# Moving 128 rows of w_down into eight small late loads, and a back-edge mark on VectorE's loop, in a decode kernel that mixes attention and a feed-forward block

## The chip, the cores and the metric

The kernel runs on one core of one Trainium2 chip. The metric is the device time of one execution in microseconds (us); before the change it is 350.62 us, the median of three runs (350.5 to 350.71).

## The reference

One token `x` of 512 numbers goes through an attention block with cached keys and values and through a feed-forward block; a gate mixes the two results.

```python
g = _sigmoid((x * gate_w).sum(-1, keepdims=True))
a = _A_ref(x, A_k_cache, A_v_cache, A_wq, A_wo)   # 32 query heads, 8 K/V heads, 32768 positions, head size 128
b = _B_ref(x, B_w_gate, B_w_up, B_w_down)         # (silu(x @ w_gate) * (x @ w_up)) @ w_down, 512 -> 1792 -> 512
return g * a + (1 - g) * b
```

Everything is bf16. K and V together are 128 MiB, of 148.11 MB that are read in all. `w_down` has 1792 rows of 512 numbers (1 KB each).

## The kernel before

The code is written per engine, with semaphores set by hand; nothing is scheduled by a planner. All loads but two small ones (`x` and `gate_w`, on ScalarE's queue) are issued by SyncE (SP), in this order: `wq`, `w_gate`, `w_up`, then K and V of the eight K/V heads ("groups") in turn, then `w_down`, then `wo`. They go into five pages of 32 KB per partition: `PG_A`, `PG_B`, `PG_C` (0 to 2) hold K, two pages at a time, `PG_V` and the one above it V. The last V goes to `PG_B` and `PG_C`, whose K is used up first. SP waits in its own order until the page of the next load is free: for K on `sem_fill` (transposes done by TensorE), for V on `sem_v_free` (the matmuls with V done).

TensorE (PE) runs a start part, the loop over the groups and an end part. In the loop (`emit_k`) it transposes K, eight blocks to a unit (L348, `emit_fill`; sixteen units a group, each adds 1 to `sem_fill`, so that 128 means the last unit of the last group); VectorE copies each unit to SBUF (L712); PE multiplies it with the queries (L360, `emit_scores`). ScalarE makes the exponentials, and PE multiplies those of the group before with V (L417, `emit_v`).

The feed-forward block runs in the start part: gate and up products, the product `tmask`, and its transposition into columns by 14 matmuls with a vector of ones (L524), which VectorE copies to `tT` (L693). `w_down` lies as 14 consecutive rows to a partition, `wd[128, 14, 512]`, so column `j` of `tT` belongs to `wd[:, j, :]`:

```python
sp.dma_start(
    wd[:, :, :], B_w_down.rearrange("(p j) n -> p j n", j=FC)
).then_inc(sem_ld_wd, 16)
```

Its product stands in the end part (`emit_end`): after the last V product and its reduction, PE waits for `sem_ld_wd` and runs 14 matmuls of 128x1 by 128x512, `emit_strip` (L220), over four strips of one PSUM bank in turn, as partial sums onto which the first sixteen row blocks of `wo` are added. `wo` comes in five pieces (`WO_CUTS`, L340) of 16, 9, 4, 2 and 1 rows per partition, issued when the matmuls with the last but one V are done; PE uses the last four with `emit_rows` (L231) as they land. Behind the last piece VectorE copies the result row (L765), and SP and ScalarE store a half each.

Of the kernel before, what the change touches and what calls it, by code (L numbers as in the profile page):

```python
# [8 lines left out]
BF16 = mybir.dt.bfloat16  # L9
# [3 lines left out]
def bass_gated_mix__gqa_block_cached__swiglu_ffn__decode_kernel(  # L13
# [14 lines left out]
    G = A_k_cache.shape[1]  # L28
# [4 lines left out]
    F = B_w_gate.shape[1]  # L33
    NOUT = A_wo.shape[1]
# [3 lines left out]
    FC = F // 128  # L38
# [8 lines left out]
    UPG = NB * UPP  # L47
# [4 lines left out]
    STEP = 16  # L52
# [10 lines left out]
    NSTRIP = 4  # L63
# [5 lines left out]
    PG_A, PG_B, PG_C = 0, 1, 2  # L69
# [5 lines left out]
    NPG = 5  # L75
    assert G % 2 == 0

    with ExitStack() as es:
        def S_(name):
            return es.enter_context(nc.semaphore(name))  # L80
# [8 lines left out]
        sem_ld_x = S_("s_ld_x")  # L89
        sem_ld_g = S_("s_ld_g")  # L90
        sem_ld_wd = S_("s_ld_wd")
        sem_ones = S_("s_ones")
        sem_dc = S_("s_dc")
        sem_pz = S_("s_pz")
# [16 lines left out]
        sem_dve_tT = S_("s_dve_tT")  # L111
        sem_fill = S_("s_fill")
# [24 lines left out]
        def T(name, shape, dt):  # L137
            return es.enter_context(nc.sbuf_tensor(name, shape, dt))
# [5 lines left out]
        ones_bf = T("ones_bf", [128, 2], BF16)  # L144
# [8 lines left out]
        og_col = T("og_col", [128, 1], FP32)  # L153
        qblk = T("qblk", [128, (G + 2) * STEP], BF16)
        qcur = T("qcur", [128, 2, 2 * HPG], BF16)
        tT = T("tT", [128, FC], BF16)
        wd = T("wd", [128, FC, NOUT], BF16)
        page = T("page", [128, NPG, PAGE], BF16)
        ktT = T("ktT", [128, NKT, 2 * UW], BF16)
        ET = T("ET", [128, NT, HPG], BF16)  # L160
# [21 lines left out]
        ps_m = P("ps_m", [128, 512], FP32)  # L182
# [3 lines left out]
        M_P0 = M_B0 + HPG  # L186
        M_S0 = M_P0 + HPG
        M_T0 = M_S0 + HPG
        M_O0 = M_T0 + FC
        M_X0 = M_O0 + WOJ  # L190
        M_G0 = M_X0 + KC
        assert M_G0 + 1 <= 512
# [13 lines left out]
        tmask = ktT[:, 2, 0:F]  # L206
# [5 lines left out]

        wq_v = page[:, PG_Q, 0 : KC * H * DH].rearrange("p (c n) -> p c n", c=KC)
        wgu = page[:, PG_F, 0 : 2 * KC * F].rearrange("p (w c f) -> p w c f", w=2, c=KC)
        wo_v = page[:, PG_X, 0 : WOJ * NOUT].rearrange("p (j n) -> p j n", j=WOJ)
        qall = qblk[:, :].rearrange("p (g e c) -> p g e c", e=2, c=2 * HPG)

        def emit_strip(pe, w, vec, j, start, stop):
            c = j % NSTRIP
            return pe.matmul(  # L220
                ps_c[32 * c : 32 * c + 1, :],
                vec[:, j : j + 1],
                w[:, j, :],
                start=start,
                stop=stop,
                skip_group_check=True,
            )
# [32 lines left out]
        with nc.Block("main") as block:  # L260
# [25 lines left out]
            @block.sync  # L286
            def _(sp):
                def load_k(g):
                    lo = PG_A if g % 2 else PG_B
                    dst = page[:, lo : lo + NB, :].rearrange("p b (r d) -> p b r d", d=DH)  # L290
                    src = A_k_cache[0, g, :, :].rearrange("(p b r) d -> p b r d", b=NB, r=R)
                    if g > 1:
                        sp.wait_ge(sem_fill, UPG * (g - 1) + UPP)
                        sp.dma_start(
                            dst.rearrange("p b r d -> p (b r d)"),
                            src.rearrange("p b r d -> p (b r d)"),
                        ).then_inc(sem_k[0], 16)
                        return
                    for b in range(NB):
                        first = lo + b == PG_B  # L300
                        if g and first:
                            sp.wait_ge(sem_fill, UPP)
                        sp.dma_start(dst[:, b, :, :], src[:, b, :, :]).then_inc(
                            sem_k[0] if first else sem_k1 if g else sem_k[1], 16
                        )

                def load_v(g):
                    src = A_v_cache[0, g, :, :].rearrange("(p b r) d -> p b r d", b=NB, r=R)
                    if g == G - 1:
                        lo, sem = PG_L, sem_vl  # L310
                        sp.wait_ge(sem_fill, UPG * g + UPP)
                    else:
                        lo, sem = PG_V, sem_v
                        if g:
                            sp.wait_ge(sem_v_free, STEP * (g + 1))
                        else:
                            sp.wait_ge(sem_pe_h, 1)
                    sp.dma_start(
                        page[:, lo : lo + NB, :].rearrange("p b n -> p (b n)"),
                        src.rearrange("p b r d -> p (b r d)"),  # L320
                    ).then_inc(sem, 16)

                sp.dma_start(wq_v, A_wq.rearrange("(p c) n -> p c n", c=KC)).then_inc(sem_q, 16)  # L323
                for w, src in enumerate((B_w_gate, B_w_up)):
                    sp.dma_start(  # L325
                        wgu[:, w, :, :], src.rearrange("(p c) f -> p c f", c=KC)
                    ).then_inc(sem_f, 16)
                load_k(0)
                for g in range(1, G):
                    load_k(g)  # L330
                    load_v(g - 1)
                load_v(G - 1)
                sp.dma_start(
                    wd[:, :, :], B_w_down.rearrange("(p j) n -> p j n", j=FC)
                ).then_inc(sem_ld_wd, 16)
                sp.wait_ge(sem_v_free, STEP * G)
                src = A_wo.rearrange("(p j) n -> p j n", j=WOJ)
                for k, s in enumerate(sem_wo):
                    a, b = WO_CUTS[k], WO_CUTS[k + 1]
                    sp.dma_start(wo_v[:, a:b, :], src[:, a:b, :]).then_inc(s, 16)  # L340

            @block.tensor
            def _(pe):
# [103 lines left out]
                def emit_start():  # L447
                    pe.wait_ge(sem_r, 9)
                    pe.wait_ge(sem_ones, 2)
                    for n, (a, b) in enumerate(  # L450
                        ((r_row[:, 0, :], ones_f[0:1, :]), (ones_f[0:1, :], r_row[:, 1, :]))
                    ):
                        ins = pe.matmul(ps_i, a, b, start=(n == 0), stop=(n == 1))
# [4 lines left out]
                    for c in range(KC):  # L458
                        ins = pe.matmul(
                            ps_m[:, M_X0 + c : M_X0 + c + 1],  # L460
                            xv[:, c, :],
                            ones_bf[0:1, 0:1],
                            start=True,
                            stop=True,
                        )
# [4 lines left out]
                    for t in range(QT):  # L470
                        for c in range(KC):
                            for k in range(NSTRIP):
                                n = (t * NSTRIP + k) * QN
                                ins = pe.matmul(  # L474
                                    pst[0][32 * k : 32 * k + 1, t * QN : (t + 1) * QN],
                                    xT[:, c : c + 1],
                                    wq_v[:, c, n : n + QN],
                                    start=(c == 0),
                                    stop=(c == KC - 1),
                                    skip_group_check=True,  # L480
                                )
# [6 lines left out]
                        start=True,  # L488
                        stop=True,
# [6 lines left out]
                    for e in range(2):  # L496
                        for t in range(QT):
                            for j in range(NSTRIP):
# [4 lines left out]
                                    start=True,  # L503
# [15 lines left out]
                                )  # L519
                    ins.then_inc(sem_pe_h, 1)  # L520
                    pe.wait_ge(sem_dve_tm, 1)
                    tv = tmask.rearrange("p (m j) -> p j m", j=FC)
                    for j in range(FC):
                        ins = pe.matmul(  # L524
                            ps_m[:, M_T0 + j : M_T0 + j + 1],
                            tv[:, j, :],
                            ones_bf[:, 0:1],
                            start=True,
                            stop=True,
                        )  # L530
                    ins.then_inc(sem_pe_t, 1)
                    pe.wait_ge(sem_ps0, 1)
                    pe.wait_ge(sem_dve_tT, 1)
                    for n, sem in enumerate((sem_v_free, sem_red)):
                        c = M_P0 + HPG * n
                        pe.matmul(
# [16 lines left out]
                def emit_end():  # L553
                    emit_v(
                        [[(sem_exp, (G + 1) * STEP), (sem_vl, 16)], []], (PG_L, PG_L + 1)
                    )
                    pe.wait_ge(sem_rc, G * STEP)
                    emit_reduce((G + 1) * STEP)
                    pe.wait_ge(sem_ld_wd, 16)
                    for j in range(FC):  # L560
                        emit_strip(pe, wd, tT, j, j < NSTRIP, False)

                    pe.wait_ge(sem_dve_oT2, 1)
                    pe.matmul(
                        ps_m[:, M_O0 : M_O0 + WOJ], pmat[:, :], O2a[:, :], start=True, stop=True
                    ).then_inc(sem_pe_O2, 1)
                    pe.wait_ge(sem_dve_O2, 1)
                    emit_wo(pe, 0)
# [42 lines left out]
            def _(dve):  # L611
# [78 lines left out]
                    ALU.mult,  # L690
                ).then_inc(sem_dve_tm, 1)
                dve.wait_ge(sem_pe_t, 1)
                dve.tensor_copy(tT[:, :], ps_m[:, M_T0 : M_T0 + FC]).then_inc(sem_dve_tT, 1)  # L693

                def emit_out(i, at):
                    dve.wait_ge(sem_red, i + STEP)
# [8 lines left out]
                        ALU.mult,  # L705
                    ).then_inc(sem_rc, STEP)

                with dve.Fori(0, G * STEP, STEP) as i:
                    for n in range(UPG + 1):
                        if n < UPG:  # L710
                            dve.wait_ge(sem_fill, i + (n + 1))
# [47 lines left out]
        for k in range(1, len(sem_wo)):  # L759
            ins = emit_wo(pe, k)  # L760
# [37 lines left out]
```

## Time and profile before

| what | value |
|---|---|
| time, median of three runs | 350.62 us (350.5 to 350.71) |
| the profiled execution | 350.62 us, of it the span 349.3 us |
| mean granted clock of TensorE | 0.859 |
| busy: PE, weight loads of PE, VectorE, ScalarE | 258.6, 219.7, 186.3, 33.4 us |
| read from HBM | 148.11 MB, 424 GB/s over the span |
| `w_down`, issue to landing | 31.0 us |
| five pieces of `wo`, issue to landing | 18.2, 20.6, 21.4, 21.6, 21.5 us |

The span goes from the first to the last instruction of the program. Lines are named L and their number in the kernel before. "DMA share" is the mean busy share of the core's 16 DMA engines. Besides loads, the profile lists packets of kind "instruction", with which the engines' programs are fetched.

### The profile page before, as it was taken

The numbers are of one execution on the slowest core, as the hardware profiler recorded it, in microseconds if no ns is written. First come the engines' busy times: TensorE is split into PE (matmuls) and PEld (weight loads), VectorE is DVE, ScalarE is ACT, GpSimd is POOL, SyncE is SP. The second block draws the span as 40 slices with busy tenths as digits, with TensorE's granted clock in tenths as the row PEclk, the third lists the DMA queues.
The fourth block names the chain that finished last, engine by engine and source line by source line (L and its number), as shares of the span: only waits on it lengthen the run. The fifth ranks groups of instructions, "written<-read, shape, count | busy, mean of one in ns | idle before, by whom it ended". The sixth has DMA issues, their size and how long they took to land.

```text
span 349.3 us, 8833 instructions
## 1 busy us (share of the span) xinstructions
PE 258.6 (74%) x3915; PEld 219.7 (63%) x3915; DVE 186.3 (53%) x227; ACT 33.4 (10%) x143; POOL 2.8 (1%) x15
## 2 busy tenths in 40 slices
PE   1354994799749981999469982999479972999384
PEld 1124993799449941997259942996279842995241
DVE  4044994499229921697129921895139920894101
ACT  1002000300030003000400003000400012000400
POOL 3000000000000000000000000000000000000000
PEclk9996999599969987699859985898859995898878
DMA  8999999999999999999999999999999999999895
GB/s 321 417 461 420 418 430 462 453 413 428 420 443 443 428 435 443 428 443 413 435 450 428 435 413 435 450 435 428 420 435 450 428 428 420 443 443 428 388 427 236
DMA packets 3907, 148.22 MB, mean 424 GB/s; under 512 B 442, under 2 KB 572, under 8 KB 828
## 3 DMA queue, kind: packets, MB, share of 16 engines
q1 hardware_dynamic: 3892, 148.11, 98.5%
q8 instruction: 6, 0.10, 0.1%
q14 instruction: 1, 0.01, 0.0%
q10 hardware_dynamic: 8, 0.00, 0.0%
HBM read 148.11 MB, written 0.00 MB: 424 GB/s over the span
## 4 chain that ended last, share of the span: by engine, by line
DMA 61%; PE 34%; issue 2%; DVE 2%; SPq 1%; DVEq 0%
DMA page<-in_A_k_cache_dram 54%; PE pst L348 25%; DMA page<-in_A_wo_dram 6%; PE ps_sc L360 6%; DVE ktT L712 2%; PE ps_o L417 2%; SPq L340 0%; SPq L325 0%; DVE pmaxf L720 0%; PE ps_sc L231 0%; PE ps_m L401 0%; SPq L323 0%; PE ps_m L397 0%; DVE res_row L765 0%; DVE gm L730 0%
## 5 line engine op out<-in xcount | busy, mean ns | idle before, releaser
L712 DVE COPY ktT<-pst 128x2048 bf16<-128x2048 bf16 x128 | 153.4, 1221 | 66.0 <-PE pst L348 61.9
L348 PE MATMUL pst<-ident_f,page 128*128 128x128 f32 x1024 | 148.0, 300 | 40.1 <-DMA page<-in_A_k_cache_dram 37.6
L348 PEld LDWEIGHTS pst<-ident_f,page 128*128 128x128 f32 x1024 | 126.7, 155 | 44.4 <-DMA page<-in_A_k_cache_dram 38.2
L360 PEld LDWEIGHTS ps_sc<-qcur,ktT 128*128 128x128 bf16 x2048 | 64.0, 97 | 8.1 <-DVE ktT L712 7.1
L360 PE MATMUL ps_sc<-qcur,ktT 128*128 128x8 bf16 x2048 | 64.3, 166 | 6.4 <-DVE ktT L712 6.4
L417 PE MATMUL ps_o<-page,ET 128*16 128x512 bf16 x512 | 37.2, 456 | 6.0 <-DMA page<-in_A_v_cache_dram 6.0
L417 PEld LDWEIGHTS ps_o<-page,ET 128*16 128x16 bf16 x512 | 13.9, 103 | 25.5 <-issue 16.9
L599 ACT ACTIVATE ET<-ps_sc,nbias 128x128 bf16 x64 | 23.9, 556 | 52.6 <-DVE nbias L738 52.6
L592 ACT ACTIVATE acc<-ps_o 128x512 f32<-128x512 f32 x8 | 4.8, 597 | 221.2 <-PE ps_o L417 217.1
L730 DVE TENSOR_REDUCE gm<-ps_m 4x1 f32<-4x128 f32 x8 | 2.2, 278 | 39.4 <-PE ps_m L397 39.4
L599 ACT ACTIVATION_READ_ACCUMULATOR ET<-ps_sc,nbias 128x1 f32 x64 | 18.3, 285 | 0.0
L720 DVE TENSOR_REDUCE pmaxf<-ps_sc 128x4 f32<-128x512 f32 x16 | 11.0, 686 | 8.4 <-PE ps_sc L360 8.4
L474 PE MATMUL pst<-page,xT 128*1 128x512 bf16 x32 | 3.6, 627 | 9.1 <-DMA page<-in_A_wq_dram 9.1
L438 PE MATMUL ps_m<-sel,acc 128*128 128x4 f32 x64 | 8.4, 255 | 1.8 <-ACT acc L592 1.6
L438 PEld LDWEIGHTS ps_m<-sel,acc 128*128 128x128 f32 x64 | 7.7, 191 | 2.5 <-ACT acc L592 2.2
L401 PE MATMUL ps_m<-diag,ones_f 4*128 4x4 f32 x16 | 3.2, 268 | 6.9 <-DVE diag L734 6.9
L697 DVE RECIPROCAL rS<-ps_m 128x4 f32<-128x4 f32 x9 | 1.6, 182 | 12.4 <-PE ps_m L438 12.4
L401 PEld LDWEIGHTS ps_m<-diag,ones_f 4*128 4x128 f32 x16 | 2.7, 213 | 8.4 <-issue 8.4
L474 PEld LDWEIGHTS pst<-page,xT 128*1 128x1 bf16 x32 | 0.9, 115 | 10.9 <-issue 10.9
L650 DVE CAST ktT<-pst 128x1024 bf16<-128x1024 f32 x2 | 2.4, 1218 | 8.7 <-PE pst L474 8.7
L429 PEld LDWEIGHTS ps_m<-esum,ones_f 128*128 128x128 f32 x32 | 4.2, 190 | 3.5 <-issue 3.5
L429 PE MATMUL ps_m<-esum,ones_f 128*128 128x4 f32 x32 | 4.9, 258 | 0.0
(70 smaller groups left out, 48.5 us busy)
## 6 DMA issues: line engine op xcount, KB each, us to landing
page<-in_A_k_cache_dram SPq DMA_DIRECT2D x4, 4096.0 KB, 35.0
page<-in_A_wq_dram SPq DMA_DIRECT2D x1, 4096.0 KB, 13.5
page<-in_A_wo_dram SPq DMA_DIRECT2D x1, 2048.0 KB, 18.2
page<-in_B_w_gate_dram SPq DMA_DIRECT2D x1, 1792.0 KB, 17.4
page<-in_B_w_up_dram SPq DMA_DIRECT2D x1, 1792.0 KB, 21.2
wd<-in_B_w_down_dram SPq DMA_DIRECT2D x1, 1792.0 KB, 31.0
page<-in_A_wo_dram SPq DMA_DIRECT2D x1, 1152.0 KB, 20.6
page<-in_A_wo_dram SPq DMA_DIRECT2D x1, 512.0 KB, 21.4
```

The lines of the kernel that those rows point to most:

```text
L348: ins = pe.transpose(pst[u % NST][:, k * 128 : (k + 1) * 128], kv[:, n * 128 : (n + 1) * 128], ident_f[:, :],)
L360: ins = pe.matmul(ps_sc[b][:, col : col + 2 * HPG], kt[:, k, e, :], qcur[:, e, :], start=(e == 0), stop=(e == 1),)
L401: pe.matmul(ps_m[:, M_B0 : M_B0 + HPG], ones_f[0:HPG, :], diag[:, :], start=True, stop=True,).then_inc(sem_b, STEP)
L417: ins = pe.matmul(ps_o[32 * c : 32 * c + RQ * HPG, :], ET[:, n : n + RQ, :].rearrange("p n h -> p (n h)"), v[:, k * RQ : (k + 1) * RQ, :], ...
L429: pe.matmul(ps_m[:, M_S0 : M_S0 + HPG], ones_f[:, :], esum[:, b, :], start=(b == 0), stop=(b == NB - 1),)
L438: ins = pe.matmul(ps_m[:, M_P0 : M_P0 + HPG], acc[:, q, :], sel4[:, q * HPG : (q + 1) * HPG], start=(q == 0), stop=(q == RQ - 1),)
L474: ins = pe.matmul(pst[0][32 * k : 32 * k + 1, t * QN : (t + 1) * QN], xT[:, c : c + 1], wq_v[:, c, n : n + QN], start=(c == 0), stop=(c == ...
L592: act.activation(part, ps_o[:, :], ACT.Copy).then_inc(sem_acc, STEP)
L599: act.activation(ET[:, b * R : (b + 1) * R, h], sc[:, h, bass.ds(bank, R)], ACT.Exp, bias=nbias[:, h : h + 1], scale=SCALE, accum_out=esum ...
L650: dve.tensor_copy(qrow[:, r, :, :, :], pst[0][:, 0 : QT * QN].rearrange("p (x w e) -> p x e w", w=64, e=2),).then_inc(sem_dve_qT, 1)
L712: dve.tensor_copy(ktT[:, n % NKT, :], pst[n % NST][:, :].bitcast(BF16)).then_inc(sem_cp, 1)
L720: dve.tensor_reduce(pmaxf[:, b, :], sc, AX.X, ALU.max).then_inc(sem_d, 1)
```

## The change

Three things change.

`wd` keeps the first 1664 rows of `w_down`, as 13 consecutive rows to a partition. The last 128 rows go to the first page, `PG_A`, into partitions 0 to 31, four rows (4 KB) to a partition. Eight loads bring them, each to four partitions that lie eight apart (q, q + 8, q + 16, q + 24). SP issues them after the large load, once `sem_fill` has reached 128, that is, once the last K is transposed and the page free, and before it waits for the pages of `wo`.

The columns follow: 13 matmuls make `tT`, four more with 32 outputs make `tX`, and VectorE copies the two separately. In the end part 13 strips run over `wd` and four over the page, after a wait for the eight loads (`sem_ld_wx` at 128); the strip counter goes on from 13.

VectorE's loop over the groups, `dve.Fori`, becomes the same loop with `hint_back_edge=True`: one instruction at the head of the body, run every turn, that names the branch back to the head.

```diff
+    XQ, XE, FX = 8, 4, 4
+    XP = XQ * XE
+    FM = FC - XP * FX // 128
+    FR = 128 * FM
...
-        tT = T("tT", [128, FC], BF16)
-        wd = T("wd", [128, FC, NOUT], BF16)
+        tT = T("tT", [128, FM], BF16)
+        tX = T("tX", [XP, FX], BF16)
+        wd = T("wd", [128, FM, NOUT], BF16)
...
+        wx = page[0:XP, PG_A, 0 : FX * NOUT]
+        wx_v = wx.rearrange("p (i n) -> p i n", i=FX)
...
-        def emit_strip(pe, w, vec, j, start, stop):
-            c = j % NSTRIP
+        def emit_strip(pe, w, vec, j, start, stop, at=0):
+            c = (at + j) % NSTRIP
...
                 sp.dma_start(
-                    wd[:, :, :], B_w_down.rearrange("(p j) n -> p j n", j=FC)
+                    wd[:, :, :], B_w_down[0:FR, :].rearrange("(p j) n -> p j n", j=FM)
                 ).then_inc(sem_ld_wd, 16)
+                sp.wait_ge(sem_fill, UPG * G)
+                rest = B_w_down[FR:F, :].rearrange("(e q i) n -> q e (i n)", q=XQ, i=FX)
+                for q in range(XQ):
+                    sp.dma_start(wx[q:XP:XQ, :], rest[q]).then_inc(sem_ld_wx, 16)
                 sp.wait_ge(sem_v_free, STEP * G)
...
-                    tv = tmask.rearrange("p (m j) -> p j m", j=FC)
-                    for j in range(FC):
-                        ins = pe.matmul(
-                            ps_m[:, M_T0 + j : M_T0 + j + 1],
...
+                    for c, n, lo, hi, m in ((M_T0, FM, 0, FR, 128), (M_T0 + FM, FX, FR, F, XP)):
+                        tv = tmask[:, lo:hi].rearrange("p (m j) -> p j m", j=n)
+                        for j in range(n):
+                            ins = pe.matmul(
+                                ps_m[0:m, c + j : c + j + 1],
...
-                    pe.wait_ge(sem_dve_tT, 1)
+                    pe.wait_ge(sem_dve_tT, 2)
...
                     pe.wait_ge(sem_ld_wd, 16)
-                    for j in range(FC):
+                    for j in range(FM):
                         emit_strip(pe, wd, tT, j, j < NSTRIP, False)
+                    pe.wait_ge(sem_ld_wx, 16 * XQ)
+                    for j in range(FX):
+                        emit_strip(pe, wx_v, tX, j, False, False, at=FM)
...
-                dve.tensor_copy(tT[:, :], ps_m[:, M_T0 : M_T0 + FC]).then_inc(sem_dve_tT, 1)
+                dve.tensor_copy(tT[:, :], ps_m[:, M_T0 : M_T0 + FM]).then_inc(sem_dve_tT, 1)
+                dve.tensor_copy(
+                    tX[:, :], ps_m[0:XP, M_T0 + FM : M_T0 + FM + FX]
+                ).then_inc(sem_dve_tT, 1)
...
-                with dve.Fori(0, G * STEP, STEP) as i:
+                with nc.Fori(0, G * STEP, STEP, engines=(dve.engine,), hint_back_edge=True) as i:
```

## The prediction, made before the changed kernel ran

> **What bounds the kernel now.** I read the page first, and on it how full the DMA engines are.
>
> ```profile
> span 349.3 us, 8833 instructions
> PE 258.6 (74%) x3915; PEld 219.7 (63%) x3915; DVE 186.3 (53%) x227; ACT 33.4 (10%) x143; POOL 2.8 (1%) x15
> ...
> q1 hardware_dynamic: 3892, 148.11, 98.5%
> q8 instruction: 6, 0.10, 0.1%
> q14 instruction: 1, 0.01, 0.0%
> q10 hardware_dynamic: 8, 0.00, 0.0%
> ```
>
> No compute engine is above 74%, while the packets of the load queue q1 fill 98.5% of the 16 DMA engines' span. Then I asked for windows: one whole turn of the loop (the length of one K and one V group), and the stretch up to 345.0.
>
> ```profile
> 254.88:293.60 38.72, 29.64 (x463) 26.55 (x463) 21.76 (x25) 3.59 (x17) 0.00 (x0) 0.85 1.00 433
> ...
> 332.30:345.00 12.70, 9.39 (x115) 4.25 (x115) 0.98 (x5) 1.19 (x2) 0.00 (x0) 0.84 1.00 418
> ```
>
> The last two columns are the DMA share and GB/s. Share 1.00 at 433 GB/s is 27.1 GB/s for each engine, or 37.8 ns for 1 KB on one engine. The change loads the same bytes, so the end can move in two ways only: by how evenly the 16 engines finish, and by what follows the last landing. The second is the end of the chain of waits in order of time:
>
> ```profile
> 325.31 21.62 DMA page<-in_A_wo_dram
> 346.94 0.04 issue
> 346.98 0.66 PE ps_sc L231 x9
> 347.64 0.02 issue
> 347.67 0.29 DVE res_row L765
> ```
>
> The last pieces of `wo` land, and matmuls, a copy and the store follow. For the first, short windows at the end:
>
> ```profile
> 344.60:345.00 0.40, 0.14 (x8) 0.00 (x0) 0.00 (x0) 0.00 (x0) 0.00 (x0) 1.00 1.05 399
> 345.00:345.40 0.40, 0.36 (x28) 0.36 (x32) 0.00 (x0) 0.00 (x0) 0.00 (x0) 1.00 0.71 269
> 345.40:345.80 0.40, 0.33 (x24) 0.15 (x12) 0.00 (x0) 0.00 (x0) 0.00 (x0) 1.00 0.51 190
> 345.80:346.20 0.40, 0.00 (x0) 0.00 (x0) 0.00 (x0) 0.00 (x0) 0.00 (x0) 1.00 0.44 166
> 346.20:346.60 0.40, 0.29 (x16) 0.23 (x16) 0.00 (x0) 0.00 (x0) 0.00 (x0) 0.96 0.35 120
> 346.60:346.90 0.30, 0.14 (x11) 0.00 (x0) 0.00 (x0) 0.00 (x0) 0.00 (x0) 0.50 0.05 17
> ```
>
> All engines are busy until 345.0. Between 345.8 and 346.2 the share is 0.44, which is 7 of 16: nine engines are done, seven are late. After 345.0 the 16 engines together work 16 x ((0.71 + 0.51 + 0.44 + 0.35) x 0.4 + 0.05 x 0.3) = 13.1 us. The seven work 1.2 us each up to 346.2 and 2.5 us together behind it, so on average they end at 346.55, the last at about 346.8. The other nine share 13.1 - 8.4 - 2.5 = 2.2 us and end at 345.25 on average. The page has seven packets of instructions in the span (six in q8, one in q14), and seven engines are late by 1.3 us: I read it as one fetch on each of seven engines, whose delay a queue that never runs dry carries to the end. Engines that finished together would stop at 345.0 + 13.1 / 16 = 345.82, so 0.98 us is all that evening out can bring.
>
> **The change, part by part.**
>
> **The large load.** `wd` shrinks from 14 to 13 rows of 1 KB per partition, and each engine serves eight partitions: 8 KB less for every engine, 8 x 37.8 ns = 0.30 us earlier for all behind it in the queue, `wo` included.
>
> **The eight loads.** They bring back 128 KB. Each has four rows of 4 KB. How many engines serve four rows, the trace does not show; it shows one and two: q10 has eight packets in all, for two loads of one row and a store of two rows (one packet and one count each, then two and two), so one engine for each row. By that a load takes four engines. If all eight take the same four, these get 32 KB, 32 x 37.8 ns = 1.21 us; if the loads go round, all 16 get 8 KB, 0.30 us. Between these ends I take the same four, since the one-row loads give no sign of a transfer cut finer than its rows, and nothing in the code names a turn; both stay in the cases. The Trainium skill (DMA: Bandwidth & Descriptors, "Why a DMA increments its semaphore by 16 and not by 1") states that such a load uses the largest number up to 16 that divides its slowest dimension, and always the lowest-numbered engines: the same four. No run here shows the numbering.
>
> What a small load costs beside its bytes, I take from the last pieces of `wo`:
>
> ```profile
> page<-in_A_wo_dram SPq DMA_DIRECT2D x1, 512.0 KB, 21.4
> page<-in_A_wo_dram SPq DMA_DIRECT2D x1, 256.0 KB, 21.6
> page<-in_A_wo_dram SPq DMA_DIRECT2D x1, 128.0 KB, 21.5
> ...
> 323.99 2.23 SPq L340 DMA_DIRECT2D page<-in_A_wo_dram  x5
> ...
> 346.98 0.14 PEld L231 LDWEIGHTS ps_sc<-page,O 128*32 128x32 bf16 x8 [0.44 <-DMA page<-in_A_wo_dram]
> 347.31 0.11 PEld L231 LDWEIGHTS ps_sc<-page,O 128*32 128x32 bf16 x4 [0.20 <-DMA page<-in_A_wo_dram]
> ```
>
> The 128 KB piece lets PE go on 0.33 us after the one before it, and its bytes need 0.30 us at 433 GB/s: 0.03 us too much. Eight loads make 0 to 0.24 us for the four engines, and I take the upper end because the pieces are smaller still. So the four gain 1.21 + 0.24 - 0.30 = 1.15 us of work (0.91 without the excess), the other twelve lose 0.30. The seven late ones would stop at 346.5 at the latest. An early engine at the nine's mean of 345.25 would stop at 346.4, one of the latest, 345.8, at 346.95. The end moves by between -0.30 and +0.15 us if the four are all among the nine; I take -0.2, nearer to the mean.
>
> Here a rule speaks against the change, and the row above it. The row says 0.03 us per queued load. The Trainium skill (DMA: Bandwidth & Descriptors, "Rules for kernel authors") says that under 64 KB a transfer pays mostly overhead, and its fit has about 2 us for each. By it eight loads would come to some 16 us; the trace disagrees, with 0.33 us from one queued piece to the next.
>
> **The wait and SP's queue.** The loads wait until `sem_fill` is 128, the last transpose of the last K group, and behind them on SP stand the five loads of `wo`.
>
> ```profile
> SPq L340 <- PE ps_o L417: 17.3, 1, 17.3
> ...
> 314.22 1.95 PE L348 MATMUL pst<-ident_f,page 128*128 128x128 f32 x16
> ...
> wd<-in_B_w_down_dram SPq DMA_DIRECT2D x1, 1792.0 KB, 31.0
> ```
>
> SP sits idle for 17.3 us ahead of `wo`, until 323.99. The fills end at 316.17; eight issues at 2.23 / 5 = 0.45 us are done by 319.8. Free, with 4 us to spare. Were that cover gone, the queue itself would hide another ten: `wd`, issued at 306.3, lands 31.0 us later, at 337.3, and only then are the pieces of `wo` on the engines. The new strips land at 337.3 - 0.3 + 1.2 to 1.45, about 338.5.
>
> **TensorE's end.**
>
> ```profile
> 340.06 1.03 PE L220 MATMUL ps_sc<-wd,tT 128*1 128x512 bf16 x14
> 340.98 0.21 DVE L752 STREAM_TRANSPOSE O2a<-oTs 128x32 bf16<-128x32 bf16 x1
> 341.25 0.19 PE L564 MATMUL ps_m<-O2a,pmat 128*128 128x32 bf16 x1 [0.17 <-DVE O2a L752]
> 342.32 1.03 PE L220 MATMUL ps_sc<-page,O 128*1 128x512 bf16 x16 [0.88 <-DMA page<-in_A_wo_dram]
> ```
>
> The strips start at 340.06, 1.5 us after the new data is there: the new wait ends at once. Seventeen strips for fourteen add 3 x 1.03 / 14 = 0.22 us; 0.17 us of it fills PE's wait for L564. Some 0.05 us reach the next step, where PE waited 0.88 us for `wo`, of which the change takes 0.3. Nothing reaches the end.
>
> **The start.** The mask is transposed with 17 matmuls for 14, and VectorE makes one copy more.
>
> ```profile
> 30.11 1.00 PE L524 MATMUL ps_m<-ones_bf,ktT 128*128 128x1 bf16 x14 [4.16 <-DVE ktT L686]
> 31.14 0.17 DVE L693 CAST tT<-ps_m 128x14 bf16<-128x14 f32 x1 [1.09 <-PE ps_m L524]
> 32.63 4.44 PE L348 MATMUL pst<-ident_f,page 128*128 128x128 f32 x24 [0.19 <-DMA page<-in_A_k_cache_dram]
> ...
> 76.31:100.00 23.69, 17.63 (x317) 14.67 (x314) 13.18 (x18) 3.59 (x17) 0.00 (x0) 0.94 1.01 437
> ```
>
> That is 0.21 + 0.17 = 0.4 us, and PE waited 0.19 us for K anyway, so the first group starts 0.2 us later. Its successor's load, issued at 76.31, finds a full queue (share 1.01), which hides it.
>
> **The mark on VectorE's loop.** One more instruction per turn, eight in all. The trace has none; the nearest rows are VectorE's largest gap put down to issue and its idle time.
>
> ```profile
> 60.51 0.17 DVE L725 COPY qcur<-qblk 128x16 bf16 x1 [0.38 <-issue]
> ...
> L712 DVE COPY ktT<-pst 128x2048 bf16<-128x2048 bf16 x128 | 153.4, 1221 | 66.0 <-PE pst L348 61.9
> ```
>
> Between nothing and 0.38 us a turn, at the loop's head, where VectorE waits for PE: 61.9 us over the run. I take 0 on the path. Nor do I expect a gain, as VectorE is not in the end of the chain. What it could do is change a fetch of instructions; that is a rival.
>
> **The sum.** The profiled execution took 350.62 us, 1.32 beyond its span, and is the median of the runs: 350.62 - 0.2 = 350.4 us.
>
> **The rivals.**
>
> 1. *One of the four is a late engine.* Nothing shown says which seven are late. An engine that stops after 346.8 - 1.15 = 345.65 now makes the end later. At the seven's mean it would stop at 347.7, 0.9 us behind today's end; at the last, 1.15; at the first, from 346.2 and without the excess, 0.3. With several of the four at risk I take +1.0: 351.6 us. For it: seven of 16 are late, and four drawn blindly would hardly miss them all. Against: fetches need not fall blindly, and the 1.15 us added fit the gap of 1.3 almost exactly.
> 2. *The loads go round all engines,* 0.30 us off and 0.30 on: no change, 350.6 us. For it, only that the trace shows no four-row load.
> 3. *A fetch more.* The mark, or six more instructions on PE, brings one more packet of instructions onto an engine that is late already: +1.3 - 0.3, 351.6 us; one on an early engine, or one fewer, changes nothing, since others stay late. Against: the trace has seven for the whole run.
> 4. *Each small load costs like a lone one,* on the engines one after the other: well above 352 us. The 0.33 us above speak against it.
> 5. *More evenness than I count,* with fewer late engines, at most 0.98 us: 349.7 us. The seven each shed 0.30 us alone, so fetches would have to go as well.
>
> **How the numbers follow.** The four early: 0.48. Rival 1: 0.32, rival 2: 0.10, rival 3: 0.04, rival 4: 0.02, rival 5: 0.04. A difference of 0.2%, 0.7 us, is about what a measurement of this kernel can tell from no change. The forecast and rival 2 lie within it, and of rival 1 the low end, 0.07: 0.65. Slower: 0.25 + 0.04 + 0.02 = 0.31; faster: rival 5, 0.04. The range goes from 350.1 (-0.30 and the runs' spread of 0.2) to 351.7 (rival 1 up to its 1.15); outside it are rivals 4 and 5 and the tail of 1. The forecast's own range is 350.1 to 350.8.
>
> **What the profile after would show.** Right: 8 x 16 KB issued between 316 and 320; in the last windows a share that stays near 1 for longer and ends 0.2 us sooner; the last piece of `wo` let go at 347.1; PE's wait at the new semaphore nil; q8 and q14 with seven packets. Wrong: a last stretch of 1 us with a share of 0.06 to 0.25, one to four engines (rival 1); the same steps as now (rival 2); eight packets of instructions (rival 3); SP still issuing at 323.99 (the cover).

## The result: 350.01 us, 0.6 us faster, and not by what I forecast

The changed kernel takes 350.01 us (median of 22 runs, 349.82 to 350.24) where the kernel before, beside it on the same chip, took 350.61 us. The ratio is 0.9978, with a 95% interval of 0.9972 to 0.9984. I had forecast 350.4 us and a range from 350.1. The sign is right and the size is not: of two large causes that work against each other, my sum had one at nothing and the other far too small. That the sign came out right is luck. One run below, of the kernel with eight engines, took 358.84 us at a granted clock of 0.649 (0.828 to 0.861 in its others) and is left out of the comparison.

The page of the kernel after, span and queues:

```profile
span 348.6 us, 8862 instructions
...
q1 hardware_dynamic: 3956, 148.11, 98.7%
q8 instruction: 6, 0.10, 0.1%
```

The span is 0.7 us shorter. The load queue is as full as before. Of the seven packets of instructions six are left; the line of q14 is gone.

The timeline of the kernel after (start, duration, engine, line; idle time ahead of it in brackets):

```profile
315.70 5.07 SPq L349 DMA_DIRECT2D page<-in_B_w_down_dram  x8
...
323.50 2.28 SPq L354 DMA_DIRECT2D page<-in_A_wo_dram  x5
...
332.11 5.26 PE L431 MATMUL ps_o<-page,ET 128*16 128x512 bf16 x56 [5.30 <-DMA page<-in_A_v_cache_dram]
...
339.55 1.02 PE L230 MATMUL ps_sc<-wd,tT 128*1 128x512 bf16 x13
...
340.50 0.38 PE L230 MATMUL ps_sc<-page,tX 32*1 32x512 bf16 x4
...
340.82 0.19 PE L582 MATMUL ps_m<-O2a,pmat 128*128 128x32 bf16 x1
...
341.75 1.03 PE L230 MATMUL ps_sc<-page,O 128*1 128x512 bf16 x16 [0.74 <-DMA page<-in_A_wo_dram]
...
346.59 0.11 PEld L241 LDWEIGHTS ps_sc<-page,O 128*32 128x32 bf16 x4 [0.18 <-DMA page<-in_A_wo_dram]
```

The same step in the timeline of before, the first matmuls with the last V:

```profile
333.11 5.20 PE L417 MATMUL ps_o<-page,ET 128*16 128x512 bf16 x64 [6.01 <-DMA page<-in_A_v_cache_dram]
```

Both kernels wait here for a landing of V, so these rows show how far the load queue has come. After is 1.00 us ahead at this point (332.11 against 333.11), before a single byte of the moved rows has been loaded. From here to the last piece of `wo` it takes 346.59 - 332.11 = 14.48 us; before it took 347.31 - 333.11 = 14.20. So the change *gains* 1.0 us where it changes nothing and *loses* 0.28 us where I had forecast a gain of 0.2.

The lost part can be seen in one window, the stretch in which the eight small loads are on the engines (last columns: granted clock, DMA share, GB/s). First before, then after:

```profile
332.30:338.00 5.70, 4.89 (x64) 1.91 (x64) 0.00 (x0) 0.00 (x0) 0.00 (x0) 0.65 1.03 436
```

```profile
332.30:338.00 5.70, 5.70 (x67) 2.20 (x59) 0.00 (x0) 0.08 (x1) 0.00 (x0) 0.65 1.02 381
```

The share is the same and 55 GB/s are missing: the engines are as busy as before and move less, so single packets take longer. I call this the dip. 5.70 us x 55 / 436 is 0.72 us of all 16 engines. In the records of the packets, those of 16 KB take up to 1079 ns there and 611 ns a little later.

The short windows at the end of after:

```profile
344.60:345.00 0.40, 0.40 (x36) 0.30 (x24) 0.00 (x0) 0.00 (x0) 0.00 (x0) 1.00 0.72 279
345.00:345.40 0.40, 0.08 (x8) 0.00 (x0) 0.00 (x0) 0.00 (x0) 0.00 (x0) 1.00 0.63 243
345.40:345.80 0.40, 0.18 (x14) 0.18 (x16) 0.00 (x0) 0.00 (x0) 0.00 (x0) 1.00 0.63 230
345.80:346.20 0.40, 0.22 (x16) 0.05 (x4) 0.00 (x0) 0.00 (x0) 0.00 (x0) 1.00 0.24 79
346.20:346.60 0.40, 0.30 (x10) 0.13 (x11) 0.00 (x0) 0.00 (x0) 0.00 (x0) 0.96 0.00 0
```

Where before had a share of 0.44, seven engines, it now has 0.63: ten engines work up to 345.8. In the records of the last piece of `wo`, six engines land at 344.87 to 345.20 and ten at 346.05 to 346.55; before it was nine and seven. The landings of the last V, ahead of the small loads, tell how many were late already: six engines (ten at 330.25 to 330.64, six at 331.62 to 331.98), where before had seven (nine and seven). By this count the ten are six late ones and the four that took the small loads. In all 13 profiles in which no small load comes ahead of the last V, the engines that are late there are as many as the page has packets of instructions, six or seven.

### The profile page after: what moved, and what is told of

The parts are those of the page before. It is cut to its first block, busy times and chain, and to the rows that moved or that the text cites. A ratio compares the mean times of both kernels' runs of the same rounds, so it can differ in the third digit from the quotient of the medians.

```text
span 348.6 us, 8862 instructions
## 1 busy us (share of the span) xinstructions
PE 260.4 (75%) x3921; PEld 220.0 (63%) x3921; DVE 185.9 (53%) x228; ACT 33.4 (10%) x143; POOL 2.8 (1%) x15
## 4 chain that ended last, share of the span: by engine, by line
DMA 59%; PE 35%; DVE 3%; issue 2%; SPq 1%; ACT 0%; DVEq 0%
DMA page<-in_A_k_cache_dram 46%; PE pst L362 25%; PE ps_sc L374 6%; DMA page<-in_A_wo_dram 6%; DMA page<-in_B_w_up_dram 6%; PE ps_o L431 2%; DVE ktT L733 1%; PE pst L526 1%; DVE ktT L704 1%; SPq L354 0%; PE ps_m L539 0%; PE ps_m L551 0%; DVE pmaxf L741 0%; DVE ktT L695 0%; DVE ktT L693 0%
## 5 line engine op out<-in xcount | busy, mean ns | idle before, releaser
L362 PE MATMUL pst<-ident_f,page 128*128 128x128 f32 x1024 | 146.5, 298 | 40.7 <-DMA page<-in_A_k_cache_dram 38.0
L362 PEld LDWEIGHTS pst<-ident_f,page 128*128 128x128 f32 x1024 | 125.3, 153 | 45.0 <-DMA page<-in_A_k_cache_dram 38.5
L431 PE MATMUL ps_o<-page,ET 128*16 128x512 bf16 x512 | 39.5, 478 | 5.3 <-DMA page<-in_A_v_cache_dram 5.3
L431 PEld LDWEIGHTS ps_o<-page,ET 128*16 128x16 bf16 x512 | 15.0, 108 | 26.1 <-issue 19.0
```

The source lines that it names most:

```text
L362: ins = pe.transpose(pst[u % NST][:, k * 128 : (k + 1) * 128], kv[:, n * 128 : (n + 1) * 128], ident_f[:, :],)
L431: ins = pe.matmul(ps_o[32 * c : 32 * c + RQ * HPG, :], ET[:, n : n + RQ, :].rearrange("p n h -> p (n h)"), v[:, k * RQ : (k + 1) * RQ, :], ...
```

## The experiments

Ratios are against the kernel before, run beside each on the same chip (medians 350.6 to 350.7 us).

**The mark alone** (before, with only the loop's head changed).

```diff
-                with dve.Fori(0, G * STEP, STEP) as i:
+                with nc.Fori(0, G * STEP, STEP, engines=(dve.engine,), hint_back_edge=True) as i:
```

> The kernel before with the back-edge mark on VectorE's loop alone; w_down is loaded as before. Theory A (evenness: the eight loads take 8 KB, 0.30 us, from every late engine, and the mark does nothing): 350.6 us, -0.0 to -0.1, seven packets of instructions. Theory B (the mark takes the 8 KB fetch of instructions away, which the profile after no longer shows, and with it a delay at the front of the stream): -0.3 to -0.6 us, six packets of instructions. Theory C (the loop's large packets last 2418 ns in the profile after for 2421 to 2428 before, 0.15%, some 0.4 us over the run; whoever shortens them): if the mark does it, 2418 here and -0.3 to -0.4 us.

350.64 us, ratio 0.9998 [0.9989, 1.0007]. The page has six packets of instructions and no q14. At the last V six engines are late instead of seven, and the last landing stays where it was (347.35 against 347.27). The mark removes a fetch, and by itself the fetch costs nothing.

**The loads alone** (after, with the old loop head).

> The changed kernel with VectorE's loop unmarked, as before; the eight loads stay. Theory A: all of the gain, -0.5 to -0.7 us. Theory B: what is left without the mark, -0.0 to -0.3 us, and seven packets of instructions again. In both, the stretch in which the small loads run shows lengthened packets on all engines, as in the profile after (16 KB packets of wo at about 1.0 us for 0.61).

350.48 us (350.32 to 351.06), ratio 0.999 [0.9977, 1.0003], 0.47 us more than after (349.82 to 350.24). q14 is back. The end windows of this kernel:

```profile
345.80:346.20 0.40, 0.40 (x23) 0.40 (x19) 0.00 (x0) 0.00 (x0) 0.00 (x0) 0.50 0.13 46
346.20:346.60 0.40, 0.40 (x24) 0.40 (x20) 0.00 (x0) 0.00 (x0) 0.00 (x0) 0.50 0.06 23
346.60:347.00 0.40, 0.40 (x28) 0.40 (x20) 0.00 (x0) 0.00 (x0) 0.00 (x0) 0.50 0.05 18
```

A share of 0.06 is one engine that works alone; its last piece lands 2.38 us behind the first. At the last V seven engines are late; at the last piece of `wo` six are early, nine are some 1.3 us later and one is later still. That is the count if one of the four that take the small loads is also one of the seven: 9 - 3, 7 - 1 + 3, and 1. So here my rival 1 came true, by one engine, and the mark matters beside the loads, though not alone.

**One load over all engines** (after, with the 128 rows in a single load of 32 partitions).

```diff
-                for q in range(XQ):
-                    sp.dma_start(wx[q:XP:XQ, :], rest[q]).then_inc(sem_ld_wx, 16)
+                sp.dma_start(
+                    wx[0:XP, :], B_w_down[FR:F, :].rearrange("(p i) n -> p (i n)", i=FX)
+                ).then_inc(sem_ld_wx, 16)
```

> The changed kernel with the 128 rows in one load of 32 rows of 4 KB, which 16 engines share evenly; mark, wait, strips and page as changed. Theory A (evenness): late engines lose 8 KB and get 8 KB back, so 0.3 to 0.6 us worse than the changed kernel, 350.3 to 350.6 us. Theory B (mark): as good as the changed kernel, 350.0 us. If the dip of the DMA rate around the small loads is due to four engines' 4 KB rows, it is gone here and the time may even be lower, 349.7 us.

350.23 us (349.80 to 351.18), ratio 0.9989 [0.9979, 0.9999]; the profiled execution took 350.89. Its windows:

```profile
332.30:338.00 5.70, 5.70 (x65) 2.04 (x58) 0.00 (x0) 0.00 (x0) 0.00 (x0) 0.62 1.03 389
338.00:345.00 7.00, 4.40 (x54) 2.31 (x54) 0.98 (x5) 1.19 (x2) 0.00 (x0) 1.00 0.98 372
```

The dip does not hang on small loads over four engines: here 16 engines take two rows each, and it is there all the same. Behind it most 16 KB packets of `wo` stay at 681 to 684 ns; why they stay slow I did not settle.

**Before again**, unchanged, one run.

> The kernel before, profiled on the same chip as the others. Theory C needs the large packets at 2421 to 2428 ns here and at 2418 in one of the changed ones; if they last the same in all profiles of this chip, the 0.15% was the chip or the run and not the change.

350.55 us. The 64 KB packets of K and V take 2422.6 ns on average (here and below without the few above 2430 ns), in the first profile of before 2422.4. In after they take 2418.1 ns, so that difference belongs to the kernel, not to the run.

**Before, with its tiles 32 bytes further on.** `wd` and the pages begin, in each partition, at bytes 23776 and 38112 in before and at 23808 and 37120 in after: the new tile `tX` moved all behind it up by 32 bytes, and the `wd` that is one row shorter moved the pages down by 1024. Both starts of after are multiples of 256, those of before are not. This kernel gives before an unused tile of 32 bytes, and nothing else:

```diff
         tT = T("tT", [128, FC], BF16)
+        T("pad", [128, 16], BF16)
         wd = T("wd", [128, FC, NOUT], BF16)
```

> The kernel before with an unused tile of 32 bytes per partition ahead of wd and nothing else: wd and page start at an address divisible by 64 (38144 for page) where before they started 32 bytes off (38112). Theory D (the place: the changed kernel's smaller wd and added tX put page at 37120, divisible by 64, and every load into it runs a little faster): large packets at 2418 ns as in the three kernels with the small wd, for 2422.5 on average in the three with the old one; 142 such lengths per engine by 4.5 ns, 350.0 us. Theory E (the loads themselves or the smaller wd make the stream faster): 2422 ns and 350.6 us.

349.37 us (349.27 to 349.65), ratio 0.9954 [0.9937, 0.9971]. One unused tile makes the old kernel 1.2 us faster, and faster than the changed one. Its timeline and window:

```profile
332.05 5.96 PE L418 MATMUL ps_o<-page,ET 128*16 128x512 bf16 x64 [7.06 <-DMA page<-in_A_v_cache_dram]
```

```profile
332.30:338.00 5.70, 5.70 (x65) 2.09 (x57) 0.00 (x0) 0.00 (x0) 0.00 (x0) 0.60 1.02 437
```

The last V is there at 332.05, like after's 332.11: this is the 1.0 us that after gains ahead of its own loads. The packets take 2418.0 ns. Each engine gets 112 of them: 112 x 4.4 ns is 0.49 us. Over all packets of the load queue, lengthened ones included, the records add up to 343.91 us for each engine in before and 342.99 here, 0.92 less. The fetches of instructions are shorter too (behind the first one, 881 to 961 ns for 16 KB, against 1018 to 1099 in before), and the first group begins 0.27 us sooner. I had expected 350.0 us; the gain is twice that, and what is left of it beyond the 0.92 I have not itemised.

**After, 32 bytes further on:** the same unused tile in the changed kernel, so that its tiles lose their place (`wd` 23840, pages 37152).

> The changed kernel with the same 32 bytes ahead of wd, which puts wd and page 32 bytes off a multiple of 64 again. Theory D: large packets at 2421 to 2428 ns, the gain of the stream gone, 350.5 to 350.8 us. Theory E: as the changed kernel, 350.0 us.

351.33 us, ratio 1.0017 [1.0004, 1.003]. I had expected 350.5 to 350.8. The packets are back at 2422.5 ns. Its rows:

```profile
332.85 5.02 PE L432 MATMUL ps_o<-page,ET 128*16 128x512 bf16 x64 [6.19 <-DMA page<-in_A_v_cache_dram]
```

```profile
332.30:338.00 5.70, 5.15 (x66) 2.06 (x66) 0.00 (x0) 0.02 (x1) 0.00 (x0) 0.70 0.99 356
```

So the change as it is described, without its accidental move of the tiles, makes this kernel about 0.7 us slower. Against the kernel before with the good place it is the same: 350.01 - 349.37 = 0.64 us.

**Before at two more places:** 96 bytes on (pages at a multiple of 64, not of 128) and 160 bytes on (of 128, not of 256), one run each.

> As the kernel before with 96 unused bytes ahead of wd: page at 38208, divisible by 64 but not by 128. If 64 bytes are what matters, 2418 ns per large packet; if it is 128 or more, 2421 to 2428 ns.

> As the kernel before with 160 unused bytes ahead of wd: page at 38272, divisible by 128 and not by 256. At 64 but not 128 (e8) large packets lasted 2421.7 ns on average, at 256 (e5) 2418. If 128 bytes do, 2418 ns and about 349.4 us; if it must be 256, 2421 to 2423 ns and about 350.7 us.

350.78 and 350.22 us; packets 2421.7 and 2421.6 ns. 64 is not enough. With 128 the packets are a mixture of 2418, 2422 and 2426 ns, and one time of 350.22 us doesn't tell whether a part is gained. Only the multiples of 256 gave the whole.

Here a rule of the Trainium skill bears. Under DMA: Bandwidth & Descriptors, "How a descriptor splits into AXI transactions", it says that a transfer is cut at boundaries of 256 bytes, and that a start off the boundary costs one cut piece more, and the beats of 32 bytes that are fetched in vain. The runs agree on the boundary. On the price they speak against a count of beats: before begins 224 bytes behind a boundary (seven vain beats), the shifted after 32 (one), and they have 2422.4 and 2422.5 ns; the Trainium skill's beats would give, at 2418 ns for 2048 of them, an estimate of 8.3 and 1.2 ns more. A fixed price for the extra piece would fit, but the Trainium skill gives none there and no run shows the pieces. It tells of reads; here it is the place written to that was moved.

**The small loads earlier** (after, with a tile of their own and issued ahead of the last V, with no wait for K's page).

```diff
+        wx = T("wx", [XP, FX * NOUT], BF16)
...
+                rest = B_w_down[FR:F, :].rearrange("(e q i) n -> q e (i n)", q=XQ, i=FX)
+                for q in range(XQ):
+                    sp.dma_start(wx[q:XP:XQ, :], rest[q]).then_inc(sem_ld_wx, 16)
                 load_v(G - 1)
```

> The changed kernel with the eight small loads in a tile of their own, issued ahead of the last V load and without the wait; place of wd and page as in the changed kernel. Theory F (the small loads slow all engines' packets while they run beside the pieces of w_down and wo, which costs the end 0.55 us and eats what evenness brings): no lengthened packets of 13 KB and 16 KB, the four engines and the late ones shifted by their 0.9 and 0.3 us all the same, 0.3 to 0.6 us better than the changed kernel: 349.4 to 349.7 us. If small loads cost as much beside the 64 KB packets of the stream: 350.0 us.

349.87 us, ratio 0.997 [0.9959, 0.9981], near to after's 350.01, and above the 349.4 to 349.7 expected if the loads cost less there. Its timeline, the first transposes of the last group and the matmuls with the last V, and then the first of these two of after:

```profile
293.50 5.25 PE L361 MATMUL pst<-ident_f,page 128*128 128x128 f32 x24 [6.94 <-DMA page<-in_A_k_cache_dram]
...
333.07 5.07 PE L430 MATMUL ps_o<-page,ET 128*16 128x512 bf16 x64 [6.31 <-DMA page<-in_A_v_cache_dram]
```

```profile
293.42 5.38 PE L362 MATMUL pst<-ident_f,page 128*128 128x128 f32 x24 [7.90 <-DMA page<-in_A_k_cache_dram]
```

That stretch takes 39.57 us here and 332.11 - 293.42 = 38.69 in after; the end behind it is shorter by as much. The dip went with the loads, and the long 64 KB packets beside them took up to 3292 ns. So `wd` and `wo` as neighbours don't make it, nor the page of K, nor the wait.

**Each row to the partitions of its own engine.** I turn to where the rows are written. A load of 128 partitions gives each engine its fixed partitions; the Trainium skill (DMA: Bandwidth & Descriptors, "The descriptor swizzle") has two sets of four neighbours to an engine, 0 to 3 and 32 to 35 to the first, 4 to 7 and 36 to 39 to the second, and each engine's eight share a port. No run here shows the numbers themselves. I call four such neighbours a group. By this, if four engines take the rows of a small load in order, nearly all rows of the change, with partitions eight apart, go into groups that other engines are filling at that moment. So here are the same 128 rows in four loads of four 8 KB rows, to partitions q, q + 4, q + 8 and q + 12:

```diff
-    XQ, XE, FX = 8, 4, 4
+    XQ, XE, FX = 4, 4, 8
```

> The changed kernel with the same 128 rows in four loads of four rows of 8 KB: partitions 0 to 15, and a load's four rows go to q, q + 4, q + 8, q + 12 (before: 32 partitions, eight apart). wd and page start at a multiple of 256 as in the changed kernel. Theory G (the dip comes from where the rows are written: neighbouring groups of four partitions are each served by one engine in a full load, and a small load that writes into the group of another engine gets in its way): here engine e writes partitions 4e to 4e + 3, its own; no lengthened packets, evenness alone is left, 0.3 us better than the kernel before shifted by 32 bytes (349.37): 349.0 to 349.2 us. Theory H (small rows read from w_down's end are slow whatever their partitions): lengthened packets as in the changed kernel, 349.9 to 350.1 us.

349.09 us (348.99 to 349.36), ratio 0.9955 [0.9942, 0.9968]: the fastest kernel of the study. Its windows, over the loads and at the end:

```profile
332.30:338.00 5.70, 5.48 (x70) 2.49 (x63) 0.00 (x0) 0.60 (x1) 0.00 (x0) 0.77 1.02 436
...
344.20:344.60 0.40, 0.00 (x0) 0.00 (x0) 0.00 (x0) 0.00 (x0) 0.00 (x0) 1.00 0.62 241
344.60:345.00 0.40, 0.33 (x16) 0.23 (x16) 0.00 (x0) 0.00 (x0) 0.00 (x0) 1.00 0.63 228
345.00:345.40 0.40, 0.17 (x16) 0.10 (x8) 0.00 (x0) 0.00 (x0) 0.00 (x0) 0.65 0.24 79
```

436 GB/s: the dip is gone, and the 16 KB packets stay at 611 ns. The share steps down from ten engines to none as in after, 0.8 us sooner. From the last V to the last piece of `wo`, as the mean landing of the 16 engines, it takes 14.10 us here and 14.09 in the kernel before with the good place; after takes 14.88, 0.78 more.

**The same rows in one group:** four loads as in the last kernel, but each to four neighbouring partitions, so that by the Trainium skill's groups all four engines write into one.

```diff
-                rest = B_w_down[FR:F, :].rearrange("(e q i) n -> q e (i n)", q=XQ, i=FX)
+                rest = B_w_down[FR:F, :].rearrange("(q e i) n -> q e (i n)", q=XQ, i=FX)
...
-                    sp.dma_start(wx[q:XP:XQ, :], rest[q]).then_inc(sem_ld_wx, 16)
+                    sp.dma_start(wx[XE * q : XE * (q + 1), :], rest[q]).then_inc(sem_ld_wx, 16)
```

> As e9, with the four rows of a load in four neighbouring partitions (4q to 4q + 3): the same loads, sizes and rows in all, but all four engines write into the group of one. Theory G: a dip at least as long as in the changed kernel, 350.0 to 350.8 us. Theory H: the same time as e9.

350.19 us (349.46 to 350.47), ratio 0.9982 [0.9974, 0.9991], and in the window:

```profile
332.30:338.00 5.70, 5.54 (x68) 2.29 (x67) 0.00 (x0) 0.59 (x1) 0.00 (x0) 0.75 1.02 407
```

The loads have the same number, bytes and row size as in the kernel of 349.09 us; what differs is which partitions, and with them which rows of `w_down`, go into one load. The dip is back, with 16 KB packets of up to 1341 ns, but smaller than in after: 14.53 us from V to `wo`, 0.43 more than without it, where I had expected it at least as long. The time is as long all the same, since one engine lands 0.45 us behind all others, at 346.76. So neither small loads nor their bytes make a dip by themselves, and the partitions written to are the one cause that fits every kernel here. One thing is not separated: the four rows of a load follow each other in memory here and lie 32 KB apart in the kernel of 349.09 us. In after they lie 32 KB apart too and the dip is there, but its rows are of 4 KB, and no run has such rows in their own groups.

**Eight engines in place of four**, each in its own group (256 rows, `wd` with 12 blocks, tiles still at multiples of 256).

```diff
-    XQ, XE, FX = 4, 4, 8
+    XQ, XE, FX = 4, 8, 8
```

> The kernel with the rows in their own partition groups (349.09 us), with eight engines in place of four: 256 rows of w_down in four loads, each of eight 8 KB rows to partitions q, q+4, ... q+28; wd keeps 12 row blocks, all tiles still start at multiples of 256 bytes. Every engine sheds another 8 KB (0.30 us); engines 0 to 3 carry 32 KB as before, four more carry 32 KB for the first time. Theory: rows written to the group of four partitions that the engine itself serves slow nobody down, so no packet is lengthened (16 KB packets stay near 611 ns), and the end is set by evenness alone. In the run with four engines six engines ended early (344.02 to 344.51) and ten at 345.3 to 345.6. If the four new engines are all among the six, they end at 344.9 to 345.4 and the rest at 345.0 to 345.3: about 348.8 to 348.9 us. If one of them is a late engine, it ends 0.9 us later than now: 350.0 us; since six of the twelve other engines are late, this is the likelier case by far, and the last landing then shows one to four engines alone at about +2.4 us. Rival: small loads slow all engines by their bytes, wherever they write: twice the bytes, lengthened packets again, 350.5 us or more with all 16 engines later.

349.96 us, ratio 0.9968 [0.9955, 0.9982]; expected for a late engine among the new four: 350.0, and without one 348.8 to 348.9, where one of its runs lies (348.87). The end of the profiled execution (350.16):

```profile
345.00:345.40 0.40, 0.40 (x16) 0.36 (x12) 0.00 (x0) 0.00 (x0) 0.00 (x0) 0.50 0.18 67
345.40:345.80 0.40, 0.40 (x28) 0.40 (x20) 0.00 (x0) 0.00 (x0) 0.00 (x0) 0.50 0.13 51
345.80:346.20 0.40, 0.40 (x28) 0.40 (x20) 0.00 (x0) 0.00 (x0) 0.00 (x0) 0.50 0.13 46
```

A share of 0.13 is two engines, which end 2.6 and 2.8 us behind the first. At the last V ten engines are early and six late; at the last piece of `wo` it is four, ten and two, as it must be if two of the eight carried a fetch (10 - 6, 6 - 2 + 6, 2). The 16 KB packets stay at 611 ns, with twice the bytes. This is my rival 1 again, with two engines, and here eight engines bring less than four.

## Why the prediction was wrong, step by step

A chain of four kernels splits the result into three terms: the place of the tiles, -1.24 us (349.37 against 350.61); evenness at the end, -0.28 (349.09 against 349.37); rows written into other engines' groups, +0.92 (350.01 against 349.09). As steps of one chain they add up to the measured -0.60 whatever their causes. The first step differs in the place alone, the second in the mark as well, and the third also in the number and row size of the loads.

- **The step that was missing, a term at nothing: the place.** I listed what the change removes, adds and moves among instructions and bytes, and left out what the declarations of `tX` and the shorter `wd` do to the addresses of all tiles behind them. The two kernels' allocations could have been compared before any run. Without the good place the change is slower than before, 351.33 us, so the forecast of a gain was wrong for what I had reasoned about.
- **The step that failed: "What a small load costs beside its bytes".** I took 0.24 us, on the four engines alone, from pieces of `wo` that cover all 128 partitions. A load of four rows is not such a piece: where it writes matters. It cost all 16 engines 0.72 us by the missing bytes, 0.78 by their mean landing, 0.92 in time. In their own groups four loads of 32 KB cost nothing beside their bytes that the runs show. The Trainium skill's rule on transfers under 64 KB, which I set against the row, is far too high here too: some 16 us against 0.92. The fit of about 2 us behind it is given there (DMA: Bandwidth & Descriptors, "Anatomy of one DMA — SWDGE (gpsimd) path") for loads issued by GpSimd, while these are issued by SP.
- **Right, in part by luck: the large load and the same four engines.** 0.30 us off every engine, 32 KB on four that are all early: forecast -0.2, measured -0.28 once the writes are in their own groups. At the loads' semaphore the trace has five count records for each load, one soon after its issue and four with its landings; a load over all engines has 16. Rival 2 falls. Rival 1 falls for the changed kernel only: without the mark one of the four is late. That all four are early I owe to the mark, which I had put at nothing.
- **Right: the wait and the queue.** The eight issues run from 315.70 to 320.77, a little slower than my 0.45 us each, and `wo` follows at 323.50. The margin was 2.7 us rather than 4.
- **Right: TensorE's end.** The four strips start at 340.50 right behind the others, the wait of 0.17 us ahead of the next step is gone (L582), and ahead of `wo` PE still waits 0.74 us.
- **The start:** I had it 0.2 us late; PE began the first group at 32.42 (before: 32.63). Nothing hung on it.
- **The mark:** at nothing alone, as forecast. That a fetch fewer "changes nothing, since others stay late" (rival 3) holds in before and fails beside the loads, where it is worth 0.47 us, since one of the four engines is then late.
- **Rival 4** named the right suspect with the wrong mechanism: the small loads do cost more than their bytes, but by slowing the packets of all engines, not as lone loads one after the other. **Rival 5** fell: the late engines stayed late.

## What to carry to other kernels

In a kernel bound by loads, compare the start addresses of all load targets modulo 256 before and after any edit to the tiles: here one unused 32-byte tile is worth 1.2 us of 350, more than the change itself. When rows are given to a few engines to even out the end, write each engine's rows into the partitions that it serves in the large loads; here the same bytes elsewhere slowed all 16 engines. Count first which engines are late already, since a late one among the few undoes the gain. Where a change gains ahead of the place that it touches, look for what moved, and undo the move alone.

## What the runs showed of the hardware

- Loads into tiles that start off a multiple of 256 bytes took about 2422.5 instead of 2418 ns for 64 KB on one engine (2421.7 with tiles at a multiple of 64 and not of 128 bytes, 2421.6 at one of 128 and not of 256), and 612 to 621 instead of 611 ns for 16 KB. That a few ns for each packet come to more than 1 us, and that fetches of instructions shorten with it, I had not expected. Which of the moved tiles does it wasn't separated, nor what makes the 0.3 us beyond the records of the packets.
- While the changed kernel's eight loads of four rows were on the engines, the packets of all 16 engines were longer for some 2 us, 16 KB up to 1079 ns for 611, at an unchanged DMA share; with the rows in their own groups they were not. The share therefore doesn't show it; GB/s in the same window does (381 against 436). Why rows on a few partitions slow all engines stays open.
- Fetches of instructions, all of them over by 69 us, leave as many engines late by about 1 us as there are fetches, and the gap is still there at the last landing 280 us later. Where a late engine also took small loads, it ended 2.4 to 2.8 us behind the first (one engine without the mark, two in the kernel with eight engines).
